# Moving the rotation ahead of the scan from VectorE to GpSimd, and adding the split-off exponentials' exponent in f32

## The chip, the cores and the metric

One core of one Trainium2 chip runs the kernel. The metric is the device time of one execution in microseconds, the median over several runs. Engines are named as in the profile: PE is TensorE's matmuls, PEld its weight loads, DVE is VectorE, ACT is ScalarE, POOL is GpSimd, SP is SyncE.

## The reference, cut to what matters

```
g = sigmoid((x * gate_w).sum(-1))                      # x: 2048 x 1024, bf16
a = S5(x)      # diagonal complex state space, 1024 states: h[t] = Lam_bar*h[t-1] + B_bar x[t];
               # y = 2 Re(C h) + x*Dskip
b = MHA(x)     # 32 heads of 32, full softmax over 2048 keys, then @ wo
out = g*a + (1-g)*b
```

## The kernel before, in words

**Attention sets the beat.** The scores of 32 heads are worked off in 512 *bursts*. A burst is four heads of one group, 256 queries and 256 keys: eight score matmuls (`burst`, PE L1576) fill two PSUM slots of 1024 columns per partition, two exponentials on ACT (L1594) turn them into two bf16 tiles `pt`, and 16 small matmuls (`pv`, PE L1655) add the tiles' products with V into PSUM bank 6. There are three PSUM slots for scores, so that PE can run about one burst ahead of ACT. After every eight bursts `normalize` (DVE L1668, L1669) divides by the row sums.

**Everything else is filled in.** Projections for the next head group, the state space's input projection (`d_u`), its output projection (`d_c`) and the output projection (`d_out`) are *chains* of eight 512-column matmuls, four in each burst, all into the one PSUM bank 7. So a chain takes two bursts, and at its end VectorE copies bank 7 out (the evictions L1410, L1427, L1439, L1475, L1499). The next chain's first matmul waits for that copy, and PE's queue is in order: a late copy holds the next burst's scores too.

**The state space.** 32 *items*: four time chunks of 512 by eight blocks of 128 states. For each, two chains bring u (real and imaginary) into a buffer `ub`. The recurrence is complex; with the tables `Et` (cosine, sine) the input is first turned back, so that a real scan can follow, and the result is turned forward again (`item_ops`). An item of the kernel before is, all on VectorE: four bf16 products of `ub` and `Et` and two sums into f32 `ut` (L1341), two scans of 512 steps (L1350), a copy of the last column (L1353, not in the last chunk), and four products and two sums for the turn forward into `hp` (L1341). After eight items `carry` hands the state to the next chunk with six tiny operations on GpSimd (L1374).

**Exponentials on VectorE.** In some bursts the last 256 of the 1024 columns of the second slot are not done by ACT (which then runs L1591 on 768) but by VectorE and GpSimd. Such bursts come in pairs (bursts 0 and 2, or 4 and 6, of eight), worked off together as 512 columns (`x_ops`): L1585 on VectorE scales the score to a 32-bit fixed-point exponent for each burst; then L1611 on GpSimd takes the upper 16 bits as exponent field (`xe`), L1620 and L1614 on VectorE work out a cubic polynomial of the lower 16 bits, L1615 on GpSimd scales it to bf16 (`xp`), and L1618 on VectorE adds the two bit patterns. `x_pv` multiplies the result with V (L1635).

**The planner.** `build` goes through the bursts in order and writes each engine's whole instruction order beforehand. `t0` is a burst's planned start, 1.83 us after the one before (`PERIOD`); `dve_t` is the planned time up to which VectorE is filled. Items wait as a list `bg`, table and `C` scaling work (`table_ops`, `fold_ops`) as `bg2`, the exponentials' work as `xbg`; in each burst as many are issued as fit by their planned costs before the chain's copy. The next `u` chain is let in when few enough items are open (`items_done`). A pair of bursts is given to VectorE when the background lists are nearly empty (`X_MOST`). The semaphore waits follow from the order and from tokens for each buffer.

Of the kernel before, what the change touches and what calls it, by code (L numbers as in the profile page):

```python
# [935 lines left out]
X_UNITS = (9, 63)  # L936
X_MOST = 0.01
# [16 lines left out]
class FastPath:  # L954

    def __init__(self, nc, S, es, d, flag):
# [370 lines left out]
    def item_ops(self, j, ch, n):  # L1327
        dve, ub, tq, ut, ht = self.dve, self.ub, self.tq, self.ut, self.ht
        b = self.hp_of[ch]
        hp = self.hpb[b]  # L1330
# [8 lines left out]

        def tt(c, o, a, b, op, r, w):  # L1340
            ops.append((c, lambda: dve(lambda e: e.tensor_tensor(o, a, b, op), r, w)))  # L1341
        tt(0.335, t[0], ure, er, ALU.mult, [u0, Et], [k[0]])
        tt(0.335, t[1], uim, ei, ALU.mult, [u1, Et], [k[1]])
        tt(0.335, t[2], uim, er, ALU.mult, [u1, Et], [k[2]])
        tt(0.335, t[3], ure, ei, ALU.mult, [u0, Et], [k[3]])
        tt(0.6, ut[:, 0, :], t[0], t[1], ALU.add, k[0:2], [("ut", 0)])
        tt(0.6, ut[:, 1, :], t[2], t[3], ALU.subtract, k[2:4], [("ut", 1)])
        rr = self.pf[:, self.RR, j:j + 1].to_broadcast([128, 512])
        for ri in range(2):
            ops.append((1.29, lambda ri=ri: dve(lambda e: e.tensor_tensor_scan(ht[:, ri, :], rr, ut[:, ri, :], self.init[:, ri, j:j + 1], ALU.mult, ALU.add),  # L1350
                                                [("ut", ri), "init", ("pf", self.RR)], [("ht", ri)])))
        if ch < 3:
            ops.append((0.13, lambda: dve(lambda e: e.tensor_copy(self.hl[:, :, j], ht[:, :, 511]), [("ht", 0), ("ht", 1)], [("hl", j)])))  # L1353
# [248 lines left out]
    def x_ops(self, b):  # L1602
# [4 lines left out]
        bits = xp.bitcast(mybir.dt.int16)  # L1607
        w = 65536.0
        i2, p2 = [("xi", 0), ("xi", 1)], [("xp", 0), ("xp", 1)]
        dead = [("pf", i) for i in range(8, 21)] + ["iot", "ioth", "ioti"] + [("pw2", i) for i in range(2)] if b == 0 else []  # L1610
        self.pool(lambda e: e.tensor_scalar(self.xe, hi, 128.0, 0.0, ALU.mult, ALU.add), i2, ["xe"] + dead, "x_e")  # L1611

        def last():
            self.dve(lambda e: e.scalar_tensor_tensor(xq[:], xq[:], E1 / E3 * w * w, lo, ALU.add, ALU.mult), ["xq"] + i2, ["xq"], "x_q")  # L1614
            self.pool(lambda e: e.tensor_scalar(xp[:], xq[:], E3 / (w * w * w), E0, ALU.mult, ALU.add), ["xq"], p2, "x_p")  # L1615

        def out():
# [436 lines left out]
```

## Time and profile before

| what | value |
|---|---|
| median of 3 runs | 951.7 us (951.43 to 952.03) |
| the profiled execution's own time | 952.28 us |
| its span, first to last instruction | 950.5 us |
| granted TensorE clock, mean | 0.997 |
| busy: PE / ACT / DVE / POOL | 923.3 / 928.6 / 668.8 / 109.1 us |
| exponentials with 768 columns (L1591) | 114 |

The profile is of one execution. Busy time is a union, so instructions that overlap on one engine count once; a group's mean is of single instructions and holds the overlap. `idle before` is the engine's idle time right before a group's instructions, and the arrow names what ended it. In a window, the columns are the window's length and then, for each engine, busy microseconds and in brackets the number of instructions that begin there.

### The profile page before, as it was taken

What the parts mean: (1) busy time and instruction counts of PE and PEld (TensorE: products, weight loads), DVE (VectorE), ACT (ScalarE), POOL (GpSimd) and SP (SyncE); (2) the same over time, 40 slices, a digit from 0 to 9 for tenths busy, and PEclk for the clock granted to TensorE, in tenths of its full rate; (3) what the DMA queues carried; (4) which work ended last, traced back from release to release, by engine and by line L of the source; (5) the groups of instructions that cost most, each with busy time, mean ns of one, the idle gap of its engine ahead of it and who ended that gap; (6) DMA issues with size and microseconds to landing.
All of it is one profiled execution on the core that took longest, in us unless ns stands there. A gap on an engine that the chain in (4) does not pass through costs nothing.

```text
span 950.5 us, 33825 instructions
## 1 busy us (share of the span) xinstructions
PE 923.3 (97%) x15316; PEld 493.3 (52%) x15316; DVE 668.8 (70%) x1382; ACT 928.6 (98%) x1034; POOL 109.1 (11%) x154
## 2 busy tenths in 40 slices
PE   8899999999999999999999999999999999999996
PEld 4555644464444554555644655544645556444443
DVE  2788888889888767555688845588857455665664
ACT  6999999999999999999999999999999999999997
POOL 2000000000000220122200012200010222222220
PEclk9999999999999999999999999999999999999998
DMA  9668533320133102130022300133101214124312
GB/s 200 91 109 127 75 62 75 71 30 30 38 73 71 31 8 60 46 80 16 8 52 52 71 30 27 51 83 63 41 16 41 74 38 126 47 79 125 111 60 72
DMA packets 157092, 60.90 MB, mean 64 GB/s; under 512 B 145680, under 2 KB 145680, under 8 KB 156944
## 3 DMA queue, kind: packets, MB, share of 16 engines
q1 hardware_dynamic: 154784, 58.16, 27.5%
q8 instruction: 121, 1.98, 0.9%
q10 hardware_dynamic: 2160, 0.53, 0.3%
q14 instruction: 27, 0.22, 0.1%
HBM read 16.79 MB, written 12.58 MB: 31 GB/s over the span
## 4 chain that ended last, share of the span: by engine, by line
ACT 52%; PE 41%; DVE 4%; SPq 1%; DMA 1%; issue 1%; DVEq 0%
ACT f_pt L1594 45%; PE f_ps L1655 10%; PE f_ps L1462 9%; PE f_ps L1576 7%; PE f_ps L1493 5%; PE f_ps L1403 4%; PE f_ps L1421 2%; ACT f_OT L1594 2%; ACT f_Et L1594 2%; PE f_ps L1433 2%; ACT f_cT_re L1594 2%; ACT f_cT_im L1594 2%; DVE f_xT L1499 1%; SPq L1053 1%; DVE f_Ag L1475 1%; DMA f_xT<-in_A_x_dram 1%
## 5 line engine op out<-in xcount | busy, mean ns | idle before, releaser
L1594 ACT ACTIVATE f_pt<-f_ps 128x1024 bf16<-128x1024 f32 x830 | 775.8, 1164 | 6.1 <-PE f_ps L1576 2.1
L1655 PEld LDWEIGHTS f_ps<-f_V,f_pt 128*128 128x128 bf16 x7324 | 214.6, 96 | 98.8 <-issue 97.3
L1655 PE MATMUL f_ps<-f_V,f_pt 128*128 128x33 bf16 x7324 | 262.9, 178 | 0.2 <-ACT f_pt L1594 0.2
L1576 PE MATMUL f_ps<-f_Q,f_K 32*128 32x256 bf16 x4096 | 203.3, 273 | 13.9 <-ACT f_pt L1594 3.2
L1576 PEld LDWEIGHTS f_ps<-f_Q,f_K 32*128 32x128 bf16 x4096 | 60.7, 92 | 200.7 <-ACT f_pt L1594 173.9
L1433 PE MATMUL f_ps<-f_xT,f_wb 128*128 128x512 bf16 x512 | 131.0, 377 | 1.4 <-DVE f_pf L1224 0.4
L1403 PE MATMUL f_ps<-f_xT,f_wb 128*128 128x512 bf16 x464 | 119.2, 379 | 0.2
L1611 POOL TENSOR_SCALAR f_pf<-f_xi 128x512 int16<-128x512 int16 x57 | 63.8, 1119 | 407.7 <-DVE f_xi L1585 402.0
L1591 ACT ACTIVATE f_pt<-f_ps 128x768 bf16<-128x768 f32 x114 | 96.7, 848 | 1.1 <-DVE f_xi L1585 1.1
L1350 DVE TENSOR_TENSOR_SCAN f_ht<-f_pf,f_init,f_ut 128x512 bf16<-128x512 f32 x64 | 80.8, 1274 | 0.0
L1462 PE MATMUL f_ps<-f_cT_re,f_hp 128*128 128x512 bf16 x192 | 72.6, 378 | 0.6
L1462 PE MATMUL f_ps<-f_cT_im,f_hp 128*128 128x512 bf16 x192 | 72.6, 378 | 0.0
L1493 PE MATMUL f_ps<-f_wb,f_OT 128*128 128x512 bf16 x220 | 62.6, 379 | 1.4
L1421 PE MATMUL f_ps<-f_wb,f_xT 128*128 128x128 bf16 x896 | 59.2, 219 | 0.1
L1433 PEld LDWEIGHTS f_ps<-f_xT,f_wb 128*128 128x128 bf16 x512 | 40.4, 96 | 33.9 <-issue 1.5
L1585 DVE TENSOR_SCALAR f_xi<-f_ps 128x256 int32<-128x256 f32 x114 | 47.5, 417 | 14.2 <-PE f_ps L1576 13.3
L1614 DVE SCALAR_TENSOR_TENSOR f_xq<-f_xq,f_xi 128x512 f32<-128x512 f32 x57 | 55.9, 980 | 1.9
L1668 DVE RECIPROCAL f_rc<-f_ps 128x8 f32<-128x8 f32 x63 | 13.1, 208 | 62.4 <-PE f_ps L1635 41.0
L1403 PEld LDWEIGHTS f_ps<-f_xT,f_wb 128*128 128x128 bf16 x464 | 36.2, 96 | 30.0
L1439 DVE CAST f_ub<-f_ps 128x512 bf16<-128x512 f32 x48 | 33.2, 692 | 26.2 <-PE f_ps L1433 26.2
L1475 DVE TENSOR_SCALAR f_Ag<-f_ps,f_gcol 128x512 f32<-128x512 f32 x32 | 24.0, 751 | 38.3 <-PE f_ps L1462 38.3
L1421 PEld LDWEIGHTS f_ps<-f_wb,f_xT 128*128 128x128 bf16 x896 | 50.4, 97 | 1.0
(148 smaller groups left out, 893.4 us busy)
## 6 DMA issues: line engine op xcount, KB each, us to landing
ag_scratch<-f_Ag SPq DMA_DIRECT2D x32, 256.0 KB, 2.3
f_hp<-ag_scratch SPq DMA_DIRECT2D x32, 256.0 KB, 2.9
f_wb<-in_B_wqkv_dram SPq DMA_DIRECT2D x21, 256.0 KB, 4.1
out_dram<-f_xT SPq DMA_DIRECT2D x16, 256.0 KB, 2.0
f_wb<-in_B_wo_dram SPq DMA_DIRECT2D x2, 768.0 KB, 4.3
f_OT<-f_On SPq DMA_TRANSPOSE x63, 2.3
f_wb<-in_B_wqkv_dram ACTq DMA_DIRECT2D x2, 256.0 KB, 4.2
f_wb<-in_A_B_re_dram SPq DMA_TRANSPOSE x32, 3.3
```

What stands on the lines that cost most here:

```text
L1350: ops.append((1.29, lambda ri=ri: dve(lambda e: e.tensor_tensor_scan(ht[:, ri, :], rr, ut[:, ri, :], self.init[:, ri, j:j + 1], ALU.mult, ...
L1403: mms.append((1, lambda e, f, l, a=a: e.matmul(ps[:, bank, :], w[:, g % 2, part, a, :], xT[:, a, 512 * ch:512 * (ch + 1)], start=f, stop=l ...
L1421: m = e.matmul(ps[:, bank, 128 * q:128 * (q + 1)], xT[:, a, 128 * kt:128 * (kt + 1)], w[:, g % 2, 2, a, :], start=(a == 0), stop=(a == 7))
L1433: mms.append((1, lambda e, f, l, a=a: e.matmul(ps[:, 7, :], bT[:, (2 * n + ri) % 3, a, :], xT[:, a, 512 * ch:512 * (ch + 1)], start=f, sto ...
L1462: mms.append((1, lambda e, f, l, j=j, ri=ri: e.matmul(ps[:, 7, :], hp[:, ri, j, cols], cT[ri][:, j, 512 * cb:512 * (cb + 1)], start=f, sto ...
L1493: mms.append((1, lambda e, f, l, j=j: e.matmul(ps[:, 7, :], OT[:, j, 256 * qb + 128 * r:256 * qb + 128 * (r + 1)], wo[j][0][:, 512 * cb:51 ...
L1576: m = e.matmul(ps[:, 2 * sl[h // 2] + h % 2, 256 * kl:256 * (kl + 1)], K[32 * h:32 * h + 32, g % 2, 128 * kt:128 * (kt + 1)], Q[32 * h:32 ...
L1591: self.S.op("act", lambda e, s=s, p=p: e.activation(flat(self.tile[p]), flat(ps[:, 2 * s:2 * s + 2, :]), ACT.Exp, scale=SCALE), reads=[("S ...
L1594: self.act(lambda e, s=s, p=p: e.activation(self.tile[p], ps[:, 2 * s:2 * s + 2, :], ACT.Exp, scale=SCALE), [("S", s)], [("pt", p)], "exp")
L1611: self.pool(lambda e: e.tensor_scalar(self.xe, hi, 128.0, 0.0, ALU.mult, ALU.add), i2, ["xe"] + dead, "x_e")
L1614: self.dve(lambda e: e.scalar_tensor_tensor(xq[:], xq[:], E1 / E3 * w * w, lo, ALU.add, ALU.mult), ["xq"] + i2, ["xq"], "x_q")
L1655: m = e.matmul(ps[:, 6, o:o + 33], self.tile[p][:, h2, 256 * kl + 128 * qt:256 * kl + 128 * (qt + 1)], V[:, g % 2, 2 * i + kl, h, :], star ...
```

## The change

Its description in a few words: "SSM rotation ahead of the scan on GpSimd as a second planned queue; 170 blocks of exps on VectorE from burst 108 on; exponent added in f32, bits last". In the code:

1. `item_ops` is split. `pre_ops` holds the four products and two sums ahead of the scan and gives them to GpSimd, with `tq` as the only scratch: product, product, sum into `ut`'s first half, product, product, difference into its second half. `item_ops` keeps the scans, the copy and the turn forward on VectorE; the products of the turn forward now go to `hp`, to a new scratch `tp` (in `pf`, where `xe` was) and in place into `ht`.
2. The planner gets a second time line, `pool_t`, with 1.3 us for each of the six operations (`POOL_TT`). Operations are issued in order while they fit before the burst's end; a sum waits in the plan until the scan of the item before is planned (`scanned`), since `ut` is single. An item joins VectorE's list `bg` when its six are planned. The `u` chains are now let in by `pre_done`, not `items_done`, and table work carries the burst from which it may run.
3. In `x_ops` the exponent field is no longer made on GpSimd: VectorE multiplies the upper 16 bits and adds them to the polynomial in f32 (a third operation of the L1614 kind), and one GpSimd operation scales and writes the 16-bit pattern. L1611 and L1618 go.
4. The bursts that are given to VectorE stand in a list, `X_PLAN`, in place of the rule with `X_MOST`; VectorE's choice among the three lists is by the earliest start.

```diff
-X_UNITS = (9, 63)
-X_MOST = 0.01
+POOL_TT = 1.3
+X_PLAN = (168, 172, 176, 180, 184, 188, 204, 208, 212, 216, 220, 224, 228, 232, 236, 240, 244, 248, 252, 296, 300, 304, 308, 312, 316, 320, 324, 328, 332, 376, 380, 400, 404, 408, 412, 416, 420, 424, 428, 432, 436, 440, 444, 448, 452, 456, 460, 464, 468, 472, 476, 480, 484, 488, 492, 496, 500,)
...
-    def item_ops(self, j, ch, n):
...
-        tt(0.335, t[0], ure, er, ALU.mult, [u0, Et], [k[0]])
-        tt(0.335, t[1], uim, ei, ALU.mult, [u1, Et], [k[1]])
-        tt(0.335, t[2], uim, er, ALU.mult, [u1, Et], [k[2]])
-        tt(0.335, t[3], ure, ei, ALU.mult, [u0, Et], [k[3]])
-        tt(0.6, ut[:, 0, :], t[0], t[1], ALU.add, k[0:2], [("ut", 0)])
-        tt(0.6, ut[:, 1, :], t[2], t[3], ALU.subtract, k[2:4], [("ut", 1)])
+    def pre_ops(self, j, ch, n):
...
+        def tt(o, a, b, op, r, w, add=False):
+            ops.append((POOL_TT, lambda: self.pool(lambda e: e.tensor_tensor(o, a, b, op), r, w), add))
+        t = [tq[:, 0, :], tq[:, 1, :]]
+        k = [("tq", 0), ("tq", 1)]
+        tt(t[0], ure, er, ALU.mult, [u0, Et], [k[0]])
+        tt(t[1], uim, ei, ALU.mult, [u1, Et], [k[1]])
+        tt(ut[:, 0, :], t[0], t[1], ALU.add, k, [("ut", 0)], True)
+        tt(t[0], uim, er, ALU.mult, [u1, Et], [k[0]])
+        tt(t[1], ure, ei, ALU.mult, [u0, Et], [k[1]])
+        tt(ut[:, 1, :], t[0], t[1], ALU.subtract, k, [("ut", 1)], True)
+        return ops
...
-        tt(0.335, t[0], hre, er, ALU.mult, [("ht", 0), Et], [k[0]])
-        tt(0.335, t[1], him, ei, ALU.mult, [("ht", 1), Et], [k[1]])
-        tt(0.335, t[2], hre, ei, ALU.mult, [("ht", 0), Et], [k[2]])
-        tt(0.335, t[3], him, er, ALU.mult, [("ht", 1), Et], [k[3]])
...
+        tt(h0, hre, er, ALU.mult, [("ht", 0), Et], [hk[0]] + hw)
+        tt(tp, him, ei, ALU.mult, [("ht", 1), Et], ["tp"] + dead)
+        tt(h1, hre, ei, ALU.mult, [("ht", 0), Et], [hk[1]] + hw)
+        tt(him, him, er, ALU.mult, [("ht", 1), Et], [("ht", 1)])
+        tt(h0, h0, tp, ALU.subtract, [hk[0], "tp"], [hk[0]])
+        tt(h1, h1, him, ALU.add, [hk[1], ("ht", 1)], [hk[1]])
...
-        self.pool(lambda e: e.tensor_scalar(self.xe, hi, 128.0, 0.0, ALU.mult, ALU.add), i2, ["xe"] + dead, "x_e")
 
         def last():
-            self.dve(lambda e: e.scalar_tensor_tensor(xq[:], xq[:], E1 / E3 * w * w, lo, ALU.add, ALU.mult), ["xq"] + i2, ["xq"], "x_q")
-            self.pool(lambda e: e.tensor_scalar(xp[:], xq[:], E3 / (w * w * w), E0, ALU.mult, ALU.add), ["xq"], p2, "x_p")
-
-        def out():
-            self.dve(lambda e: e.tensor_tensor(bits[:], self.xe, bits[:], ALU.add), ["xe"] + p2, p2, "x_out")
+            self.dve(lambda e: e.scalar_tensor_tensor(xq[:], hi, 128.0 / X_K, xq[:], ALU.mult, ALU.add), i2 + ["xq"], ["xq"], "x_q")
+            self.pool(lambda e: e.tensor_scalar(bits, xq[:], X_K, 128.0 * (E0 + 126.0), ALU.mult, ALU.add), ["xq"], p2, "x_p")
             self.x_done.add(b)
...
-            if p % 4 == 0 and X_UNITS[0] <= p // 8 < X_UNITS[1]:
-                if sum(c for c, *_ in self.bg + self.bg2) < X_MOST:
-                    self.x_plan(p // 8, X_AT[p // 4 % 2])
+            if p % 4 == 0 and p in X_PLAN:
+                self.x_plan(p // 8, X_AT[p // 4 % 2])
...
-                            u_ok = ri == 1 or (self.items_done >= n - (3 if n < 18 else 1) and hp_free)
+                            u_ok = ri == 1 or (self.pre_done >= n - (3 if n < 18 else 1) and hp_free)
...
+            self.t1 = t0 + period
+            while self.pre:
+                n, j, ch, ready, ops = self.pre[0]
+                if n < 8 and n not in self.tabled:
+                    break
+                c, f, add = ops[0]
+                if add and len(self.scanned) < n:
+                    break
+                st = max(self.pool_t, ready, t0, self.scanned[n - 1] if add and n else 0.0)
+                if st + c > self.t1 + 0.3:
+                    break
+                f()
+                ops.pop(0)
+                self.pool_t = st + c
+                if not ops:
...
+                    self.bg += [(c, f, n) for c, f in self.item_ops(j, ch, n)]
```

More of the change, by code (lines that the diff above doesn't have):

```diff
@@ L1606, in x_ops @@
         hi = xi.bitcast(mybir.dt.int16)[:, 1::2]
[L1607 removed]
+        bits = xp.bitcast(mybir.dt.int16)[:]
         w = 65536.0
         i2, p2 = [("xi", 0), ("xi", 1)], [("xp", 0), ("xp", 1)]
[L1610 to L1611 removed]
         def last():
[L1614 to L1618 removed]
+            self.dve(lambda e: e.scalar_tensor_tensor(xq[:], hi, 128.0 / X_K, xq[:], ALU.mult, ALU.add), i2 + ["xq"], ["xq"], "x_q")
+            self.pool(lambda e: e.tensor_scalar(bits, xq[:], X_K, 128.0 * (E0 + 126.0), ALU.mult, ALU.add), ["xq"], p2, "x_p")
             self.x_done.add(b)
[L1620 to L1622 removed]
+        return [(0.66, 0.0, lambda: self.dve(lambda e: e.scalar_tensor_tensor(xq[:], lo, E2 / E3 * w, lo, ALU.add, ALU.mult), i2, ["xq"], "x_q")),
+                (0.7, 0.0, lambda: self.dve(lambda e: e.scalar_tensor_tensor(xq[:], xq[:], E1 / E3 * w * w, lo, ALU.add, ALU.mult), ["xq"] + i2, ["xq"], "x_q")),
+                (0.7, 0.0, last)]
     def x_pv(self, b):
@@ L1754, in build @@
                 if n == 1:
-                    self.xbg += [[c, wait, f] for c, wait, f in self.x_ops(b)]
+                    self.xbg += [(c, f) for c, _, f in self.x_ops(b)]
             q0, q1 = self.quarters[p]
@@ L1758, in build @@
             for b in self.x_when.get(p, ()):
-                assert b in self.x_done, p
+                while b not in self.x_done:
+                    self.xbg.pop(0)[1]()
                 self.x_pv(b)
@@ L1853, in build @@
-                if not (self.bg or self.bg2):
+                now = max(self.dve_t, t0 + 0.3)
+                todo = [(max(now, self.pre_t.get(src[0][2], 0.0) if src is self.bg else 0.0), k, src) for k, src in enumerate((self.xbg, self.bg, self.bg2)) if src and not (k == 2 and len(src[0]) > 2 and src[0][2] > p)
+                        and not (k == 1 and self.bg2 and src[0][2] not in self.tabled)]
+                if not todo:
                     break
-                src = self.bg if self.bg and (self.bg[0][2] in self.tabled or not self.bg2) else self.bg2
```

65 lines of the change are left out of this document (29 added, 36 removed).

## The prediction

> **What bounds the kernel now.** I read the page's busy shares and its chain of waits first:
>
> ```profile
> PE 923.3 (97%) x15316; PEld 493.3 (52%) x15316; DVE 668.8 (70%) x1382; ACT 928.6 (98%) x1034; POOL 109.1 (11%) x154
> ...
> ACT 52%; PE 41%; DVE 4%; SPq 1%; DMA 1%; issue 1%; DVEq 0%
> ```
>
> ACT and PE are both nearly full, and the chain alternates between them; VectorE, which the change relieves, holds 4% of it. So the table of windows matters more than the mean: whose time is full where. The first seven windows are bursts 16 to 31, 32 to 47, 48 to 63, 64 to 79, 80 to 95, 112 to 127 and 256 to 287 (the start of a burst is the start of its first exponential), all without VectorE exponentials; in the last every second burst has them.
>
> ```profile
> core 0: us, PE busy (x) PEld busy (x) DVE busy (x) ACT busy (x) POOL busy (x), PEclk, DMA share, GB/s
> 39.80:69.90 30.10, 29.66 (x530) 15.45 (x526) 24.77 (x68) 30.01 (x35) 0.00 (x0) 1.00 0.54 86
> 69.90:99.60 29.70, 29.70 (x588) 17.94 (x585) 25.24 (x51) 29.70 (x33) 0.00 (x0) 1.00 0.81 124
> 99.60:129.10 29.50, 29.41 (x562) 17.46 (x563) 25.26 (x51) 29.50 (x33) 0.00 (x0) 1.00 0.43 60
> 129.10:158.30 29.20, 28.73 (x451) 13.70 (x448) 24.74 (x51) 29.20 (x34) 0.00 (x0) 1.00 0.38 79
> 158.30:187.60 29.30, 28.53 (x452) 13.47 (x450) 26.00 (x52) 29.30 (x33) 1.68 (x6) 1.00 0.36 79
> 216.90:246.30 29.40, 29.13 (x466) 14.61 (x467) 26.42 (x53) 29.40 (x34) 0.00 (x0) 1.00 0.08 25
> 477.80:536.20 58.40, 57.37 (x950) 29.61 (x946) 51.39 (x110) 58.40 (x66) 0.00 (x0) 1.00 0.34 70
> 770.00:800.00 30.00, 29.85 (x531) 17.66 (x528) 16.52 (x33) 29.29 (x35) 6.95 (x8) 1.00 0.24 76
> ```
>
> Without VectorE exponentials ACT is busy every microsecond and VectorE 82 to 90%; with them PE is full (29.85 of 30.00) and VectorE 55%. Nowhere does VectorE set the pace, but in the first kind of window it has only 3 to 5 us left in 30, and GpSimd is empty. The waits' view bounds what relief alone can bring:
>
> ```profile
> PEld f_ps L1576 <- ACT f_pt L1594: 173.9, 418, 1.2
> ...
> PEld f_ps L1493 <- DVE f_xT L1499: 2.7, 16, 0.2
> ...
> PEld f_ps L1462 <- DVE f_Ag L1475: 2.2, 13, 0.2
> ...
> PEld f_ps L1576 <- DVE f_K L1146: 2.0, 4, 0.7
> ```
>
> PE waits for VectorE some 7 us in all, most of it in bits of 0.2 us, and 173.9/418 = 0.42 us at a time for ACT: that is PE's spare time in a burst, and it swallows copies of bank 7 that are late by less.
>
> **Part 1: the exponentials' number.** The description speaks of 170 blocks from burst 108 on. The list in the code holds 57 starts from burst 168 on, each for two bursts, so 114 blocks; following the old rule through its planner gives the same 57 starts, and the row says x114 too:
>
> ```profile
> L1594 ACT ACTIVATE f_pt<-f_ps 128x1024 bf16<-128x1024 f32 x830 | 775.8, 1164 | 6.1 <-PE f_ps L1576 2.1
> L1591 ACT ACTIVATE f_pt<-f_ps 128x768 bf16<-128x768 f32 x114 | 96.7, 848 | 1.1 <-DVE f_xi L1585 1.1
> ```
>
> ACT and PE therefore get exactly the work they had. No term of the sum comes off them.
>
> **Part 2: exponent in f32.** The rows that it touches, with those of part 3:
>
> ```profile
> L1350 DVE TENSOR_TENSOR_SCAN f_ht<-f_pf,f_init,f_ut 128x512 bf16<-128x512 f32 x64 | 80.8, 1274 | 0.0
> L1611 POOL TENSOR_SCALAR f_pf<-f_xi 128x512 int16<-128x512 int16 x57 | 63.8, 1119 | 407.7 <-DVE f_xi L1585 402.0 <-PE f_ps L1576 5.6
> L1614 DVE SCALAR_TENSOR_TENSOR f_xq<-f_xq,f_xi 128x512 f32<-128x512 f32 x57 | 55.9, 980 | 1.9
> L1620 DVE SCALAR_TENSOR_TENSOR f_xq<-f_xi 128x512 f32<-128x512 uint16 x57 | 39.5, 692 | 1.9
> L1615 POOL TENSOR_SCALAR f_xp<-f_xq 128x512 bf16<-128x512 f32 x57 | 35.2, 617 | 35.4 <-DVE f_xq L1614 35.4
> L1439 DVE CAST f_ub<-f_ps 128x512 bf16<-128x512 f32 x48 | 33.2, 692 | 26.2 <-PE f_ps L1433 26.2
> L1618 DVE TENSOR_TENSOR f_xp<-f_pf,f_xp 128x512 int16<-128x512 int16 x57 | 23.8, 418 | 11.8 <-POOL f_xp L1615 11.8
> L1341 DVE TENSOR_TENSOR f_ut<-f_tq 128x512 f32<-128x512 bf16 x32 | 21.9, 684 | 0.0
> L1319 DVE TENSOR_TENSOR f_OT<-f_OT 128x512 f32<-128x512 f32 x32 | 20.5, 684 | 0.0
> L1341 DVE TENSOR_TENSOR f_tq<-f_ub,f_Et 128x512 bf16<-128x512 bf16 x48 | 18.3, 419 | 0.0
> L1305 DVE SCALAR_TENSOR_TENSOR f_cT_re<-f_cT_re,f_pf,f_OT 128x512 bf16<-128x512 bf16 x16 | 11.9, 747 | 0.0
> L1303 DVE TENSOR_SCALAR f_OT<-f_cT_im,f_pf 128x512 f32<-128x512 bf16 x16 | 7.7, 481 | 0.0
> ```
>
> A pair of bursts costs VectorE 0.69 + 0.98 + 0.42 = 2.09 us now. After, three operations of the L1620 kind: 3 x 0.69 = 2.07 us, or 2.7 if the new one, with its strided 16-bit input, takes L1614's 0.98 each time. GpSimd loses 1.12. VectorE is at 55% there and the result is read four bursts later, so: zero, off the path. Its cover is VectorE's 13 idle us in 30; the worst case, 57 x 0.6 = 34 us, stays under that. Below zero is excluded too: the waits' view has no row in which PE waits for L1618.
>
> **Part 3: the rotation on GpSimd.** An item takes 4 x 0.42 + 2 x 0.68 = 3.04 us off VectorE, 97 us over 32 items. GpSimd gets 192 operations with two inputs of 512. The trace has none of that size, but it shows what happens when both engines want SBUF, in two places of the timeline:
>
> ```profile
> 403.15 0.69 DVE L1620 SCALAR_TENSOR_TENSOR f_xq<-f_xi 128x512 f32<-128x512 uint16 x1
> 403.20 1.12 POOL L1611 TENSOR_SCALAR f_pf<-f_xi 128x512 int16<-128x512 int16 x1 [4.80 <-DVE f_xi L1585]
> 403.87 0.98 DVE L1614 SCALAR_TENSOR_TENSOR f_xq<-f_xq,f_xi 128x512 f32<-128x512 f32 x1
> ...
> 541.39 0.76 DVE L1341 TENSOR_TENSOR f_tq<-f_ht,f_Et 128x512 bf16<-128x512 bf16 x2
> 541.57 1.32 POOL L1374 TENSOR_TENSOR f_cm<-f_hl,f_W 128x8 f32<-128x8 f32 x4 [64.29 <-DVE f_hl L1353]
> 542.07 0.76 DVE L1341 TENSOR_TENSOR f_ut<-f_ht,f_Et 128x512 bf16<-128x512 bf16 x2
> 542.86 0.47 POOL L1374 TENSOR_TENSOR f_init<-f_cm 128x8 f32<-128x8 f32 x2
> 543.06 0.69 DVE L1427 CAST f_V<-f_ps 128x512 bf16<-128x512 f32 x1 [0.23 <-PE f_ps L1421]
> ```
>
> First place: L1620 ends at 403.84; the GpSimd operation ends at 404.32, 0.48 later; L1614 starts at 403.87 and takes 0.98, which is 0.29 more than L1620. They ran in turns, each waiting for the other. Second place: beside four bf16 products, GpSimd's four tiny ones take 0.32 each (1.29 to the next group), the pace of the products themselves (541.39 to 542.07 for two); beside a copy out of PSUM two take 0.47, or 0.23 each. So an operation of VectorE with two SBUF inputs and one of GpSimd go one for one, and a copy from PSUM blocks nobody. [...] It speaks against this change: by it a rotation on GpSimd isn't beside VectorE but between its operations.
>
> The price of one: one input of 512 held VectorE off till 404.32, 0.48 us of turn. Two inputs cost between 0.48 (read together) and 2 x 0.62 = 1.23 (twice the L1615 row); I take 2 x 0.48 = 0.95, as the two products' inputs are read by an engine that took 0.48 for one. Of these turns some fall beside PSUM copies (0.69 every other burst) or idle time; in a window where VectorE is full I count five sixths as lost to it, **0.8 us an operation** (ends 0.4 and 1.2). [...]
>
> Now by windows: VectorE before, plus what the new order moves (counted in both planners' orders and priced by the rows above), plus 0.8 us for each GpSimd operation there, against the window's length, which ACT sets.
> - 64 to 79: 24.74; twelve rotation operations go (-6.1), two table operations, six scalings and four of the L1305 kind come forward from later (+1.4 +2.9 +3.0): 25.9. Sixteen on GpSimd: +12.8. 38.7 against 29.2: **9.5 late**.
> - 80 to 95: 26.0; -6.1 and nine table operations less (-6.1), but ten L1305, eight scalings and two products come: +0. Fifteen: +12.0. 38.0 against 29.3: **8.7 late**.
> - 16 to 31: six rotation operations (-3.0) and two products less (-0.8), three table operations more (+2.0): 24.77 - 1.8 + 9 x 0.8 = 30.2 against 30.1, zero. 32 to 47: twelve (-6.1), a scan and its copy (-1.4) less, three table operations and two products more (+2.9): 25.24 - 4.6 + 10 x 0.8 = 28.6 against 29.7, zero. 48 to 63: six less (-3.0), a scan, its copy and a table operation more (+2.1): 25.26 - 0.9 + 5 x 0.8 = 28.4 against 29.5, zero.
> - 112 to 127: the 29 fold operations that came forward (-18.0), six rotation operations (-3.0) and three copies of bank 7 (-2.2) go; four scans, thirteen products, six copies and two small ones come (+15.0): 26.42 - 8.2 + 13 x 0.8 = 28.6 against 29.4, zero.
> - 256 to 287: 35 rotation operations (-17.6), a scan and its copy (-1.4), six products and an L1618 (-2.9) go: 51.39 - 21.9 + 31 x 0.8 = 54.3 against 58.4, zero; 336 to 367 alike.
>
> What is late is VectorE's queue, and in it the copy of bank 7; behind that stand PE's next chain, the next scores and ACT. Nothing gives it back, since the order is fixed and ACT was full. That is 18 us. In the other windows the sum fits but not each chain: where the turn forward falls into one chain, 6 x 0.34 + 3 x 0.95 + 0.69 = 5.6 us stand against 3.66 and PE's spare 2 x 0.42, 1.1 late; for some 20 items outside the two windows, at a third of the time, 7 us. Together +25.
>
> Small things at nothing: `carry`'s six tiny operations stand behind rotations on GpSimd's queue (three times, some us, their reader is bursts away); L1615 likewise where a stretch of exponentials begins. No DMA is added, and the loads for `u` chains hang on the same evictions, SP's order with them.
>
> **The rivals.**
> 1. *Hidden.* The turns fall beside PSUM copies and VectorE's waits, 0.2 us or less of each is lost ((29.2 - 25.9)/16), and nothing is late. For: VectorE idles 3 to 13 us per window. Against: the one-for-one rows. Time: 952, within 1.5 us.
> 2. *Faster.* Rival 1's condition, and VectorE, 97 us lighter, copies out earlier, so that PE's 7 us of waiting for it go. Decides: lost turn under 0.2 us. For: those waits are real. Against: they lie mostly in windows with VectorE exponentials, where no rotation runs. Time: at best 951.7 - 7 = 945, likely 948.
> 3. *GpSimd becomes the bound.* Its operation costs its turn, 0.95 to 1.2, its own fixed 0.23 and the wait for one VectorE operation, about 0.65 as a mean of 0.42, 0.75 and 1.27: 1.83 to 2.1 against a burst's 1.83, for one operation in each burst. At 2.1 each item is 6 x 0.27 = 1.6 late, scans wait for `ut`, copies behind them: 26 items outside the two windows, +42 on top: 1019. It decides at 1.83 us an operation.
>
> **How the numbers follow.** The chance of the forecast, late copies by turns, is 0.62; hidden 0.12, faster 0.08, GpSimd the bound 0.18. The sum stands on the profiled execution, 952.28 us, 0.6 above the median; I put it on the median: 951.7 + 25 = 977. With 0.4 an operation the two windows are 3.1 and 2.7 late, and no bunching: 957. With 1.2, windows 16 to 63 give 7, 64 to 95 give 31, 112 to 127 gives 4, the two late double windows 8 each, with the 7: +65, 1017. The forecast's own range is 957 to 1017; mine reaches to 951 for the hidden case and 1020 for the third rival, leaving some 0.17 out. Within 0.2% (1.9 us, about what a measurement of this kernel can tell from no change) is 0.12, faster 0.08, slower 0.80.
>
> **What would show it.** L1591 still x114. GpSimd some 200 us busier, its new operations at a mean above 1 us. VectorE's products of the turn forward and scans longer than 0.42 and 1.27 where GpSimd runs. Bursts 64 to 95 at 2.4 us and not 1.83, with idle ACT and PE waiting for DVE evictions; windows with VectorE exponentials unchanged. Wrong: scans and products at their old means, or bursts 64 to 95 at 1.83. Right in kind but rival 3: DVE scans waiting for POOL `ut`, and windows 256 to 287 and 336 to 367 late as well.

## The result: 952 to 1040 us

Four runs of each kernel on the same chip: before 951.87 us (951.43 to 952.79), after 1040.39 us (1038.36 to 1041.63). The ratio is 1.0918, with a 95% interval of 1.0902 to 1.0933: 88 us slower, where 25 were forecast. One execution of the write-only kernel below, 1061 us at a granted clock of 0.752 where its nine others took 951 to 954, is in no ratio.

The page of the kernel after, its profiled execution at 1039.70 us: the span, the busy shares and the chain.

```profile
span 1038.0 us, 33880 instructions
...
PE 946.9 (91%) x15316; PEld 502.1 (48%) x15316; DVE 687.5 (66%) x1190; ACT 933.9 (90%) x1034; POOL 299.9 (29%) x289
...
PE 62%; DVE 23%; ACT 12%; issue 2%; SPq 1%; DMA 1%; DVEq 0%
```

The span grew by 87.5 us. PE ran as many matmuls as before, 15316, but was busy 946.9 - 923.3 = 23.6 us longer: the same work at a lower granted clock, 0.963 as a mean against 0.997. Its idle time went from 950.5 - 923.3 = 27.2 to 1038.0 - 946.9 = 91.1 us, which is the other 63.9. VectorE's share of the chain went from 4% to 23%, ACT's from 52% to 12%.

The table of windows of the kernel after. The rows are bursts 16 to 31, 32 to 47, 48 to 63, 64 to 79, 80 to 95, 112 to 127, 128 to 143, 144 to 159, 256 to 287 and 336 to 367, and last a stretch with VectorE exponentials.

```profile
core 0: us, PE busy (x) PEld busy (x) DVE busy (x) ACT busy (x) POOL busy (x), PEclk, DMA share, GB/s
...
40.00:72.40 32.40, 29.85 (x530) 15.56 (x527) 27.63 (x61) 30.11 (x35) 16.65 (x12) 1.00 0.46 78
72.40:106.70 34.30, 30.02 (x589) 18.11 (x587) 27.00 (x45) 29.86 (x33) 13.78 (x11) 1.00 0.63 109
106.70:137.80 31.10, 29.56 (x562) 17.51 (x561) 27.03 (x48) 29.49 (x33) 5.63 (x4) 1.00 0.36 56
137.80:177.90 40.10, 31.34 (x454) 14.28 (x451) 37.40 (x46) 30.42 (x33) 23.90 (x18) 0.91 0.28 57
177.90:224.60 46.70, 34.45 (x451) 14.73 (x448) 38.75 (x56) 30.14 (x34) 19.80 (x20) 0.78 0.34 61
253.60:287.80 34.20, 30.06 (x504) 16.39 (x504) 26.06 (x37) 29.87 (x33) 22.00 (x16) 0.95 0.07 13
287.80:326.90 39.10, 32.21 (x465) 15.04 (x461) 26.87 (x36) 29.79 (x33) 18.99 (x15) 0.87 0.20 45
326.90:361.80 34.90, 31.24 (x469) 15.49 (x466) 22.06 (x37) 29.50 (x33) 14.80 (x16) 0.90 0.23 58
534.80:608.00 73.20, 62.16 (x952) 31.70 (x949) 48.51 (x66) 59.65 (x66) 42.93 (x34) 0.91 0.27 55
694.60:766.50 71.90, 60.82 (x949) 32.04 (x945) 46.85 (x62) 59.40 (x65) 43.23 (x35) 0.93 0.29 57
827.00:855.00 28.00, 27.92 (x476) 15.72 (x471) 15.73 (x31) 27.50 (x33) 1.85 (x3) 1.00 0.21 64
```

The first five rows answer to 30.1, 29.7, 29.5, 29.2 and 29.3 us before, the sixth to 29.4, the ninth to 58.4; the trace of before has 29.3 for bursts 128 to 143 and for 144 to 159, and 58.4 for 336 to 367. So the losses are 2.3, 4.6, 1.6, 10.9, 17.4, 4.8, 9.8, 5.6, 14.8 and 13.5 us, 85.3 of the 87.5. Every window with rotation lost time. The last row has not: 28.00 us with 33 exponentials begun, 0.85 each, where the stretch of that kind shown of before has 30.00 with 35, 0.86 each. The row to look at is bursts 128 to 143: VectorE is busy 26.87 us of work that would fit the old 29.3, and the window takes 39.1. A sum by windows can't see that loss. Bursts 128 to 159, for which the prediction's list has no row, lost 15.4 us.

The groups of the kernel after that answer to those shown of before (mean ns behind the busy time, then the idle time ahead of the group):

```profile
L1338 POOL TENSOR_TENSOR f_tq<-f_ub,f_Et 128x512 bf16<-128x512 bf16 x96 | 123.0, 1297 | 86.1 <-DVE f_ub L1452 41.1 <-DVE f_Et L1323 40.7
L1338 POOL TENSOR_TENSOR f_ut<-f_tq 128x512 f32<-128x512 bf16 x64 | 88.0, 1375 | 158.1 <-DVE f_ht L1361 155.0
L1603 ACT ACTIVATE f_pt<-f_ps 128x768 bf16<-128x768 f32 x114 | 95.4, 837 | 1.2 <-DVE f_xi L1597 1.2
L1361 DVE TENSOR_TENSOR_SCAN f_ht<-f_pf,f_init,f_ut 128x512 bf16<-128x512 f32 x64 | 84.9, 1348 | 0.0
L1358 DVE TENSOR_TENSOR f_pf<-f_ht,f_Et 128x512 bf16<-128x512 bf16 x32 | 33.4, 1044 | 0.0
L1452 DVE CAST f_ub<-f_ps 128x512 bf16<-128x512 f32 x48 | 33.0, 687 | 28.2 <-PE f_ps L1446 28.1
L1320 DVE TENSOR_TENSOR f_OT<-f_OT 128x512 f32<-128x512 f32 x32 | 30.2, 989 | 0.0
L1365 DVE CAST f_hl<-f_ht 128x2 f32<-128x2 bf16 x24 | 17.2, 715 | 0.8
```

The turn forward's second product takes 1044 ns, not 419; a scan 1348, not 1274; the table operation L1320, not touched by the change, 989, not 684. The copies out of PSUM (L1452) stay at 687, against 692. The waiting goes the other way round than rival 3 had it: the scans' idle time is 0.0, but GpSimd waits 155 us for scans, because its sums need the one `ut` that the scan of the item before still reads.

What follows from that wait stands in the timeline of the kernel after (start, us, engine, line, operation):

```profile
170.52 2.45 DVE L1361 TENSOR_TENSOR_SCAN f_ht<-f_pf,f_init,f_ut 128x512 bf16<-128x512 f32 x2
...
171.94 1.98 POOL L1338 TENSOR_TENSOR f_ut<-f_tq 128x512 f32<-128x512 bf16 x1 [8.15 <-DVE f_ht L1361]
...
174.68 1.02 PE L1446 MATMUL f_ps<-f_xT,f_wb 128*128 128x512 bf16 x4 [0.38 <-DVE f_ub L1452]
175.35 1.37 DVE L1358 TENSOR_TENSOR f_pf<-f_ht,f_Et 128x512 bf16<-128x512 bf16 x1
...
176.51 1.22 POOL L1338 TENSOR_TENSOR f_ut<-f_tq 128x512 f32<-128x512 bf16 x1
176.64 1.38 DVE L1358 TENSOR_TENSOR f_hp<-f_ht,f_Et 128x512 bf16<-128x512 bf16 x1
...
177.81 2.50 POOL L1338 TENSOR_TENSOR f_tq<-f_OT,f_Et 128x512 bf16<-128x512 bf16 x2
177.94 1.37 DVE L1358 TENSOR_TENSOR f_ht<-f_ht,f_Et 128x512 bf16<-128x512 bf16 x1
179.23 1.37 DVE L1358 TENSOR_TENSOR f_hp<-f_hp,f_pf 128x512 bf16<-128x512 bf16 x1
...
181.25 0.68 DVE L1452 CAST f_ub<-f_ps 128x512 bf16<-128x512 f32 x1
...
182.07 1.86 PE L1446 MATMUL f_ps<-f_xT,f_wb 128*128 128x512 bf16 x4 [3.84 <-DVE f_ub L1452]
```

Read it in four steps. GpSimd's sum has waited 8.15 us for `ut` and starts at 171.94, when the first of the two scans has ended; so the operations behind it in GpSimd's queue stand beside the turn forward. Three products and a difference of the turn forward start at 175.35, 176.64, 177.94 and 179.23, 1.29 us apart, in turns with GpSimd; in the kernel before it was 0.34. Behind them in VectorE's queue stands the copy of bank 7, at 181.25, and PE waits 3.84 us for it. Then four matmuls that took 1.02 us before the wait take 1.86.

The last step is the clock, as the windows around it show it:

```profile
176.50:179.90 3.40, 1.74 (x30) 0.77 (x26) 3.40 (x4) 3.35 (x4) 3.31 (x3) 1.00 0.39 47
179.90:186.70 6.80, 4.63 (x35) 1.48 (x36) 4.38 (x10) 1.94 (x2) 0.41 (x1) 0.50 0.09 19
```

The granted clock is 0.50 for 6.8 us. Behind the start-up PE has 22 gaps of more than 1.2 us in this trace, 1.5 to 4.1 us each and 61.7 us together, about all of the added idle time (the kernel before has none); 15 of them are followed by half the clock, for 72 us in all. In these 61.7 us VectorE is busy with the turn forward for 39.2, with the awaited copies for 15.0 and with table and `C` scaling work, which is slowed as well (L1320 at 989 ns and not 684), for 10.1 (the ends of operations overlap).

### The profile page after: what moved, and what is told of

Same layout as the page of the kernel before. It is cut to its first block, busy times and chain, and to the rows that moved or that the text cites. A ratio compares the mean times of both kernels' runs of the same rounds, so it can differ in the third digit from the quotient of the medians.

```text
span 1038.0 us, 33880 instructions
## 1 busy us (share of the span) xinstructions
PE 946.9 (91%) x15316; PEld 502.1 (48%) x15316; DVE 687.5 (66%) x1190; ACT 933.9 (90%) x1034; POOL 299.9 (29%) x289
## 4 chain that ended last, share of the span: by engine, by line
PE 62%; DVE 23%; ACT 12%; issue 2%; SPq 1%; DMA 1%; DVEq 0%
PE f_ps L1662 15%; PE f_ps L1588 11%; ACT f_pt L1606 10%; PE f_ps L1474 10%; PE f_ps L1416 9%; PE f_ps L1446 7%; PE f_ps L1434 4%; PE f_ps L1505 4%; DVE f_hp L1358 4%; DVE f_ht L1361 3%; DVE f_pf L1358 3%; DVE f_ht L1358 2%; DVE f_OT L1320 2%; DVE f_ub L1452 2%; DVE f_hl L1365 1%
## 5 line engine op out<-in xcount | busy, mean ns | idle before, releaser
L1588 PE MATMUL f_ps<-f_Q,f_K 32*128 32x256 bf16 x4096 | 207.7, 278 | 9.0 <-ACT f_pt L1606 3.3
L1446 PE MATMUL f_ps<-f_xT,f_wb 128*128 128x512 bf16 x512 | 139.4, 396 | 25.9 <-DVE f_ub L1452 13.4
L1625 POOL TENSOR_SCALAR f_xp<-f_xq 128x512 int16<-128x512 f32 x57 | 35.3, 619 | 422.3 <-DVE f_xq L1624 369.6
L1338 POOL TENSOR_TENSOR f_tq<-f_ub,f_Et 128x512 bf16<-128x512 bf16 x96 | 123.0, 1297 | 86.1 <-DVE f_ub L1452 41.1
L1416 PE MATMUL f_ps<-f_xT,f_wb 128*128 128x512 bf16 x464 | 125.9, 395 | 17.9 <-DVE f_ub L1452 10.3
L1338 POOL TENSOR_TENSOR f_ut<-f_tq 128x512 f32<-128x512 bf16 x64 | 88.0, 1375 | 158.1 <-DVE f_ht L1361 155.0
L1603 ACT ACTIVATE f_pt<-f_ps 128x768 bf16<-128x768 f32 x114 | 95.4, 837 | 1.2 <-DVE f_xi L1597 1.2
L1361 DVE TENSOR_TENSOR_SCAN f_ht<-f_pf,f_init,f_ut 128x512 bf16<-128x512 f32 x64 | 84.9, 1348 | 0.0
L1446 PEld LDWEIGHTS f_ps<-f_xT,f_wb 128*128 128x128 bf16 x512 | 41.6, 98 | 63.7 <-issue 32.0
L1434 PE MATMUL f_ps<-f_wb,f_xT 128*128 128x128 bf16 x896 | 62.3, 225 | 8.6 <-DVE f_ub L1452 4.7
L1416 PEld LDWEIGHTS f_ps<-f_xT,f_wb 128*128 128x128 bf16 x464 | 37.1, 99 | 51.2 <-DVE f_ub L1452 10.7
L1434 PEld LDWEIGHTS f_ps<-f_wb,f_xT 128*128 128x128 bf16 x896 | 53.1, 101 | 10.3 <-DVE f_ub L1452 4.9
```

What stands on the lines that cost most here:

```text
L1338: ops.append((POOL_TT, lambda: self.pool(lambda e: e.tensor_tensor(o, a, b, op), r, w), add))
L1416: mms.append((1, lambda e, f, l, a=a: e.matmul(ps[:, bank, :], w[:, g % 2, part, a, :], xT[:, a, 512 * ch:512 * (ch + 1)], start=f, stop=l ...
L1434: m = e.matmul(ps[:, bank, 128 * q:128 * (q + 1)], xT[:, a, 128 * kt:128 * (kt + 1)], w[:, g % 2, 2, a, :], start=(a == 0), stop=(a == 7))
L1446: mms.append((1, lambda e, f, l, a=a: e.matmul(ps[:, 7, :], bT[:, (2 * n + ri) % 3, a, :], xT[:, a, 512 * ch:512 * (ch + 1)], start=f, sto ...
L1588: m = e.matmul(ps[:, 2 * sl[h // 2] + h % 2, 256 * kl:256 * (kl + 1)], K[32 * h:32 * h + 32, g % 2, 128 * kt:128 * (kt + 1)], Q[32 * h:32 ...
L1603: self.S.op("act", lambda e, s=s, p=p: e.activation(flat(self.tile[p]), flat(ps[:, 2 * s:2 * s + 2, :]), ACT.Exp, scale=SCALE), reads=[("S ...
```

## The experiments

The theory after this: a turn beside a product holds VectorE up for the 0.95 us that was forecast, but the time is lost by single late copies, which the wait for `ut` puts regularly behind a slowed turn forward, and PE's clock adds to each. The rivals: that the f32 exponent costs; that the new order costs without any turns; that GpSimd's writes, not its reads, are in the way; that the loss is VectorE's lost time itself, wherever it falls.

### The exponent alone

The kernel before with the new `x_ops` only:

```diff
-            self.dve(lambda e: e.tensor_tensor(bits[:], self.xe, bits[:], ALU.add), ["xe"] + p2, p2, "x_out")
+            self.dve(lambda e: e.scalar_tensor_tensor(xq[:], hi, 128.0 / X_K, xq[:], ALU.mult, ALU.add), i2 + ["xq"], ["xq"], "x_q")
+            self.pool(lambda e: e.tensor_scalar(bits, xq[:], X_K, 128.0 * (E0 + 126.0), ALU.mult, ALU.add), ["xq"], p2, "x_p")
```

> The kernel before with the exponent added in f32 alone (three VectorE operations and one on GpSimd per pair of bursts); the rotation stays on VectorE and the order of chains is the old one. Theory (the slowdown is the rotation's alone): 952 us, within 1 us; the third operation takes 0.69 us. Rival (the longer VectorE part of the exponentials is late in the windows that have them): 957 us or more, with bursts there over 1.81 us.

Measured 953.02 us against 952.63, ratio 1.0006 (0.9997 to 1.0015). The groups of this kernel:

```profile
L1617 DVE SCALAR_TENSOR_TENSOR f_xq<-f_xq,f_xi 128x512 f32<-128x512 f32 x57 | 39.4, 692 | 1.9
L1613 DVE SCALAR_TENSOR_TENSOR f_xq<-f_xi,f_xq 128x512 f32<-128x512 int16 x57 | 39.4, 692 | 1.9
```

The new operation takes 0.69 us, and the one that took 0.98 beside GpSimd's exponent field takes 0.69 too, now that the field is gone. Part 2 costs nothing.

### The order without the turns

The kernel after, with its GpSimd operations on 8 of 512 columns (the rotation is left out for the others; `ut` is cleared at the start):

```diff
-            ops.append((POOL_TT, lambda: self.pool(lambda e: e.tensor_tensor(o, a, b, op), r, w), add))
+            ops.append((POOL_TT, lambda: self.pool(lambda e: e.tensor_tensor(o[:, 0:8], a[:, 0:8], b[:, 0:8], op), r, w), add))
```

> The changed kernel with all its orders and waits, but GpSimd's 192 rotation operations work on 8 of 512 columns, so the rest of the rotation is left out. Theory (each operation's turn at SBUF holds VectorE's operations up, and with them the copy of bank 7): turns of some 0.1 us cost nothing, 952 to 957 us. Rival (the new order and its waits are slow: scans wait for GpSimd, single ut, chains let in too early): over 1000 us. If both count, in between.

Measured 952.72 us, ratio 1.0001 (0.9992 to 1.0010). Its page:

```profile
PE 890.2 (94%) x15095; PEld 493.5 (52%) x15316; DVE 590.0 (62%) x1190; ACT 928.6 (98%) x1034; POOL 103.6 (11%) x290
```

The order, the waits and the list cost nothing; and they gain nothing. VectorE is 668.8 - 590.0 = 79 us lighter than in the kernel before, and the time is the same: rival 2's gain isn't there even with the rotation all but free. (Some matmul records are missing here, x15095, so PE's busy time isn't compared.) Against this page the turns of the kernel after cost VectorE 687.5 - 590.0 = 97.5 us, 0.51 for each of 192 operations.

### The same operations on VectorE

Same places in the order, but issued to VectorE: `self.pool(` becomes `self.dve(` in that line.

> The changed kernel with the six operations of each rotation issued to VectorE at the very places where the planner had put them on GpSimd; nothing else differs. They cost VectorE 0.42 and 0.68 us each instead of one turn of about 1.2. Theory (a turn is lost to VectorE whole): faster than the changed kernel in spite of 97 us more work on VectorE: 960 to 985 us, since the planner left no place for them. Rival (VectorE's own load is what makes it late): slower than 1040 us.

Measured 961.49 us, ratio 1.0094 (1.0078 to 1.0109). The groups:

```profile
L1338 DVE TENSOR_TENSOR f_ut<-f_tq 128x512 f32<-128x512 bf16 x64 | 43.9, 685 | 0.4
L1338 DVE TENSOR_TENSOR f_tq<-f_ub,f_Et 128x512 bf16<-128x512 bf16 x96 | 39.2, 415 | 0.2
```

Here VectorE does the rotation itself, in an order planned without room for it, and the kernel is 79 us faster than with GpSimd. A product takes VectorE 0.42 us when it does it itself, and a turn of 0.95 when GpSimd does it beside a product. But VectorE's time alone doesn't explain the 79 us: it is busy for 666.7 us here, 76.7 more than with 8 columns, or 0.40 for each of the 192 operations, against 0.51 for a turn as a mean. That is 21 us between the two kernels; the rest is not VectorE's own time.

### Write only, and half the columns

GpSimd writes the same outputs at the same places but reads nothing (the rotation is left out):

```diff
-            ops.append((POOL_TT, lambda: self.pool(lambda e: e.tensor_tensor(o, a, b, op), r, w), add))
+            ops.append((POOL_TT, lambda: self.pool(lambda e: e.memset(o, 0.5), r, w), add))
```

> The changed kernel with GpSimd's 192 operations made into memsets of the same outputs behind the same waits, so the rotation is left out and GpSimd reads nothing. Theory (it is GpSimd's reading that takes turns with VectorE's second input): 952 to 957 us, products of the turn forward back at 0.42 us. Rival (any GpSimd operation of that size, its writes too, holds VectorE off): products longer by the memset's time, 970 us or more.

Measured 953.14 us, ratio 1.0003 (0.9993 to 1.0013). The groups:

```profile
L1338 POOL MEMSET f_tq<- 128x512 bf16 x128 | 64.5, 526 | 138.7 <-DVE f_ub L1452 71.3 <-DVE f_Et L1323 64.7
L1358 DVE TENSOR_TENSOR f_pf<-f_ht,f_Et 128x512 bf16<-128x512 bf16 x32 | 13.4, 419 | 0.0
L1365 DVE CAST f_hl<-f_ht 128x2 f32<-128x2 bf16 x24 | 6.8, 281 | 0.8
```

A full-size write of 526 ns leaves the products at 419 ns, as they were before the change, where GpSimd's products and sums, which read as well, have them at 1044: it is GpSimd's reads that take the turns.

Half the columns, `[:, 0:256]` in that line (the rotation of the other half left out):

> The changed kernel with GpSimd's rotation operations on 256 of 512 columns (the other half of the rotation is left out): turns of about 0.6 us, as long as the memsets of write_only, but reading SBUF. Theory (reads take turns; what is late by less than PE's spare 0.4 us a burst costs nothing): products of the turn forward longer than 0.42 us, and a loss of less than half of 88 us, 960 to 985. Rival (every lost microsecond of VectorE counts): 996, half of the loss. Rival (length alone, reads and writes alike): 953, as write_only.

Measured 965.55 us, ratio 1.0139 (1.0122 to 1.0156), at a clock of 0.999. The groups:

```profile
L1339 POOL TENSOR_TENSOR f_tq<-f_ub,f_Et 128x256 bf16<-128x256 bf16 x96 | 71.3, 757 | 99.2 <-DVE f_ub L1453 52.9 <-DVE f_Et L1324 41.8 <-POOL f_ut L1339 0.5
L1359 DVE TENSOR_TENSOR f_pf<-f_ht,f_Et 128x512 bf16<-128x512 bf16 x32 | 22.9, 717 | 0.0
```

The product's excess is 717 - 419 = 298 ns, against 625 at full size: half. The time lost is 13 us against 88: a seventh. So the price of a turn grows with its size, but the kernel's loss does not follow VectorE's lost time.

### How lateness becomes time

The dose by itself: the kernel before, GpSimd's rotation not in it, with one, two or four scans of 1.28 us added ahead of the copy of bank 7 in 22 bursts.

```diff
+LATE = set(range(33, 160, 8)) | set(range(257, 289, 8)) | set(range(337, 369, 8))
...
+                if p in LATE:
+                    for _ in range(2):
+                        self.dve(lambda e: e.tensor_tensor_scan(self.xp[:], ...), ["xq", "init", ("pf", self.RR)], [("xp", 0), ("xp", 1)], "late")
```

> The kernel before with one extra scan of 1.27 us ahead of the copy of bank 7 at the end of 22 chains (late2 had two, late4 four). If a late copy costs its lateness less PE's spare time and the clock falls only after stalls of some 2 us: 22 x 0.5 to 0.9, 963 to 973 us, with a granted clock over 0.99. If the loss is in proportion to the extra work, half of late2's: 981 us.

> The kernel before with two extra scans of 1.27 us on VectorE ahead of the copy of bank 7 at the end of 22 chains, in windows without VectorE exponentials: the copy is late by 2.5 us. If a late copy costs what is left of it after PE's spare time (some 1 us), and no more: 22 x 1.5 = 33, 985 us. If PE's clock falls after such a stall: 1000 us or more, with a granted clock under 0.99.

> The same with four extra scans: late by 5.1 us. Without an effect of the clock 22 x 4.1 = 90, 1042 us, so just 57 more than late2. With PE's clock halved for 3.4 to 6.8 us after a stall of some 4 us, another 1.5 to 3 us each: 1075 to 1110 us, with a granted clock of 0.95 or less.

Measured: one scan 966.29 us against 952.75, ratio 1.0141 (1.0124 to 1.0158); two 1010.35 against 952.68; four 1088.78 against 952.68 (one execution each for the last two, which are 58 and 136 us from the kernel before). For each late copy: 1.28 us late cost 13.5 / 22 = 0.6 us, 2.56 cost 2.6, 5.1 cost 6.2. Of the first scan slack takes up half; beyond it each us of lateness costs more than a us: the second scan 2.0 for 1.28, the third and fourth 3.6 for 2.56. The surplus goes with the granted clock, 0.997, 0.976 and 0.938. In the timeline of the kernel with two scans, two of the late places:

```profile
146.43 0.81 PE L1435 MATMUL f_ps<-f_xT,f_wb 128*128 128x512 bf16 x3 [2.45 <-DVE f_ub L1441]
...
163.27 1.49 PE L1435 MATMUL f_ps<-f_xT,f_wb 128*128 128x512 bf16 x3 [2.63 <-DVE f_OT L1441]
```

Nearly the same wait, and three matmuls take 0.81 us after the first and 1.49 after the second. The windows of seven bursts around these two:

```profile
141.87:156.68 14.81, 11.84 (x204) 6.12 (x204) 13.24 (x24) 12.97 (x16) 0.00 (x0) 1.00 0.30 67
158.49:174.52 16.03, 12.87 (x203) 6.36 (x205) 12.58 (x23) 13.07 (x15) 0.00 (x0) 0.89 0.28 62
```

Seven bursts take 7 x 29.2 / 16 = 12.8 us without a late copy. The loss of clock in the second, 0.11 of 16.03, is one piece of 3.4 us at 0.5, and it costs 16.03 - 14.81 = 1.2 us, of which 0.2 is the longer wait. By 1.0 to 1.2 a piece the 72 us at half the clock in the kernel after come to 21 to 25 us of its 88, near the 23.6 by which PE is busier.

### Moving the rotation off the turn forward

`ut` doubled, so that GpSimd's sums needn't wait for the scan of the item before; that there is room, it is held in bf16, which changes the scans' input precision and nothing else of the work (GpSimd's sums take 1363 ns against 1375):

```diff
+        uo = ut.bitcast(BF)[:, :, 512 * (n % 2):512 * (n % 2 + 1)]
...
-        tt(ut[:, 0, :], t[0], t[1], ALU.add, k, [("ut", 0)], True)
+        tt(uo[:, 0, :], t[0], t[1], ALU.add, k, [("ut", n % 2, 0)], True)
```

> The changed kernel in the same order, with ut in bf16 and two of them in the same bytes, so that GpSimd's sums for an item needn't wait for the scans of the item before. Theory (the wait on the single ut releases GpSimd just when VectorE begins the turn forward, so that up to six turns fall together ahead of one copy of bank 7): turns spread out, 975 to 1010 us. Rival (the sum of the turns counts, wherever they fall): 1035 to 1045.

Measured 1011.08 us, ratio 1.0621 (1.0604 to 1.0639). A wait and two groups of this kernel, from two views:

```profile
POOL f_ut L1339 <- DVE f_ht L1362: 64.7, 7, 32.8
```

```profile
L1362 DVE TENSOR_TENSOR_SCAN f_ht<-f_pf,f_init,f_ut 128x512 bf16<-128x512 f32 x64 | 95.2, 1507 | 0.0
...
L1359 DVE TENSOR_TENSOR f_pf<-f_ht,f_Et 128x512 bf16<-128x512 bf16 x32 | 27.6, 864 | 0.0
```

GpSimd's waits for scans fell from 25 to 7. Its turns now fall beside scans, 1507 ns and not 1348, and less beside the turn forward, 864 and not 1044. A turn taken beside a scan of 1.27 us stands against an operation that is long already; beside a product of 0.34 the same turn nearly quadruples it, to 1.29. That is 29 us back, with a third of the loss gone and no operation fewer. PE's gaps of over 1.2 us are 17 now, 45.4 us together, and VectorE is in the turn forward for 18.5 of them, not 39.2. It doesn't cure it: 58 us stay.

The other way: the plan told that a turn forward takes longer, so that VectorE is given less of it ahead of a copy. In `item_ops`' helper the planned price of one operation goes from 0.335 to 0.5; no instruction is changed, only its place.

```diff
-            ops.append((0.335, lambda: dve(lambda e: e.tensor_tensor(o, a, b, op), r, w)))
+            ops.append((0.5, lambda: dve(lambda e: e.tensor_tensor(o, a, b, op), r, w)))
```

> The changed kernel with the planner's price of a product or sum of the turn forward at 0.50 instead of 0.335 us, nearer to the 0.8 that they take beside GpSimd, so that fewer of them stand ahead of a copy of bank 7. Instructions and turns are the same. Theory (lateness of single copies costs, not VectorE's lost time): 990 to 1025 us. Rival (the turns' sum costs): 1035 to 1045.

Measured 1005.76 us, ratio 1.0558 (1.0541 to 1.0576). Its group:

```profile
L1358 DVE TENSOR_TENSOR f_pf<-f_ht,f_Et 128x512 bf16<-128x512 bf16 x32 | 33.0, 1032 | 0.0
```

The turns are as dear as in the kernel after, 1032 against 1044 ns, and VectorE is busy 682.2 us against 687.5; yet 35 us come back. Fewer of these operations stand in front of a copy: PE has 15 gaps of over 1.2 us, 35.0 us together, with VectorE in the turn forward for 20.0. This falls against the rival that VectorE's lost time itself is the loss.

### More exponentials on VectorE

The description spoke of 170 blocks from burst 108 on; the code has 114. With 83 starts from burst 108 on (166 blocks), on 8 columns and on the full kernel:

```diff
-X_PLAN = (168, 172, 176, 180, 184, 188, 204, 208, ...
+X_PLAN = (108, 112, 116, 120, 124, 128, 132, 136, ...
```

> cols8 (rotation on 8 columns, so free) with the list of bursts for VectorE's exponentials grown from 57 starts to 83 (166 blocks, from burst 108 on): what the relief of VectorE could be spent on. Theory (ACT gives up 0.18 us a block, but PE is the next bound, 1.80 instead of 1.83 us a burst): 52 more blocks save 3 to 5 us, 948 to 950. Rival (ACT sets the whole time): 52 x 0.32 = 17 us, 936.

> The changed kernel with the same list of 83 starts, so the change as it was described: whole rotation on GpSimd, 166 blocks. Theory: VectorE and the turns are in the same windows now, so it is no faster than the changed kernel, 1035 to 1075 us. Rival (the described version differs in kind, more exponentials pay for the turns): under 1020.

Measured, on 8 columns: 950.35 us, ratio 0.9977 (0.9967 to 0.9987); on the full kernel 1042.39 (one execution). The same 110 us in both kernels with 8 columns, first without the added blocks, then with them:

```profile
217.00:327.00 110.00, 105.55 (x1740) 55.94 (x1766) 60.83 (x126) 110.00 (x122) 13.16 (x47) 1.00 0.18 45
```

```profile
217.00:327.00 110.00, 108.97 (x1793) 57.60 (x1790) 91.97 (x180) 108.27 (x122) 17.98 (x51) 1.00 0.21 45
```

With the blocks PE is at 108.97 of 110.00: ACT is relieved, and PE is the next bound at once. So 52 more blocks are worth 2.4 us when the rotation costs nothing, and with the rotation none is seen. No kernel here, that computes the whole reference, is faster than the one before.

## Why the prediction was wrong in size

**What held.** L1603 is x114, and the kernel with the new exponent alone is level: parts 1 and 2 were zero. GpSimd is 190.8 us busier, its operations take 1.30 and 1.38 us, and they go one for one with VectorE's two-input operations. The turn was taken as 0.95 us; the products' starts give 1.29 - 0.34 = 0.95. Copies from PSUM lost nothing (687 ns against 692). The stretch with VectorE exponentials alone is unchanged. Slower was right, at 1040 against a range to 1020.

**What was too dear.** "Five sixths lost", 0.8 us an operation: VectorE lost 0.51. By the prediction's own sum, a smaller loss should have made a faster kernel than forecast. It was 63 us slower, so the fault is not in the price.

**The step that failed: the balance by windows.** The prediction added up VectorE's work in 16 bursts, held it against the window's length, and called a sum that fits zero, with 7 us for bunching "at a third of the time". Bursts 64 to 95 came to +28.3 us for the forecast 18, all others to some +59 for the forecast 7. What counts is not the window but the one copy in two bursts: PE has some 2 x 0.42 us to spare, and in the timeline its wait for one copy behind a turn forward is 3.84. And the third of the time was a mis-sized chance. The prediction treated GpSimd's place as free against VectorE's; but with a single `ut` its sums wait for the scans, and when they are let go (171.94 in the timeline) the rest of its queue runs beside the turn forward that comes behind the scans. The timeline shows that tie, and undoing it by the doubled `ut`, or making room for it by the planner's price, is worth 29 and 35 us.

**The term that was missing: PE's clock.** The prediction counted a late copy at the time it is late. The runs with added scans show 2.6 us for 2.56, with half of the first scan's 1.28 taken up by slack, and 6.2 for 5.1; the piece at half the clock costs 1.0 to 1.2 us. For the kernel after that is some 23 us, by the busier PE (23.6) and by the pieces (21 to 25).

**The rivals.** Rival 1 (hidden) is what the kernel with 8 columns and the write-only one show, and fails on the reads. Rival 2 fails even without turns: with VectorE 79 us lighter, nothing came off. Rival 3 had the windows 256 to 287 and 336 to 367 late, which they are, by 14.8 and 13.5 us, but not by its mechanism: scans wait for nothing, idle 0.0. Its time, 1019, was nearer than the forecast's for a reason that wasn't its own. (Its 0.65 us for a wait, "as a mean of 0.42, 0.75 and 1.27", is 0.81 if each counts alike.)

**Open.** No experiment splits the 58 us that remain with the doubled `ut`. In its trace, PE's 45.4 us of gaps find VectorE in scans for 0.8 us, in the turn forward for 18.5, and in table and `C` scaling work beside GpSimd for 14.6, so scans right ahead of a copy are hardly what is left. Nor was a kernel tried that plans GpSimd's operations beside PSUM copies only.

## What to carry to other kernels

Work that two engines can only do in turns isn't moved off the first by giving it to the second: price the turn (0.95 us beside a product, 0.51 as a mean) beside the operation itself (0.42 to 0.69, 0.40 as a mean), before the move. Then follow the latest single hand-over to the engine that sets the pace, not the sum over a window, and ask which wait ties the second engine's operations to the first's: a single buffer can align them at the worst place. Where PE stands still for some 2 us or more (12 of 22 places with two scans, all 22 with four), count its clock as a cost of its own, behind the stall.

## What the runs showed of the hardware that was not expected

**The clock falls after gaps shorter than its piece.** In the kernel after, the 15 stretches at a granted clock of 0.50 that follow 15 of its 22 gaps are nine of 3.41 us and six of twice that. With two added scans, gaps of 1.8 to 2.6 us were followed by half the clock at 12 of 22 places; with four, gaps of 4.4 to 5.3 us at all 22; on half the columns, gaps of 1.2 to 1.9 us at none of 6.

Why the same gap may or may not be followed by it can be read from the traces. In the kernel after, all 31 changes of the clock, over 884 us, lie whole multiples of 3.413 us apart, so they give a grid of windows. The grid of the kernel with two scans, laid over its two late copies shown, the first pair of rows around the first, the second around the second:

```profile
141.98:145.40 3.42, 2.00 (x39) 1.00 (x35) 3.25 (x6) 3.42 (x5) 0.00 (x0) 1.00 0.19 39
145.40:148.81 3.41, 2.38 (x31) 1.15 (x32) 2.46 (x4) 1.57 (x3) 0.00 (x0) 1.00 0.36 82
...
159.05:162.47 3.42, 1.59 (x28) 0.72 (x26) 3.35 (x6) 3.34 (x4) 0.00 (x0) 1.00 0.11 22
162.47:165.88 3.41, 2.61 (x28) 1.16 (x30) 2.07 (x3) 0.53 (x1) 0.00 (x0) 0.50 0.35 74
```

The grid cuts the first gap near its middle: PE idles 1.42 us of one window and 1.03 of the next, and the clock stays. It cuts the second near its end: 1.83 us are idle in one window, and the next is at half the clock. In the kernel after, behind the start-up and ahead of the last 25 us, every window at full clock with 1.70 us or more of PE's idle time is followed by half the clock, 15 of them, and none with 1.66 or less. With two scans it is 12 windows with 1.59 us or more, and one with 1.78 that isn't followed; on half the columns no window exceeds 1.56. So about half of one window idle, 1.70 us of 3.41, was enough in the kernel after; an estimate from the two numbers is that for a gap between some 1.7 and 3.4 us it is luck where the grid cuts it.

**A copy of two columns can wait as long as a large one.** The copy of the scan's last column (L1365) took 169 ns before and 715 in the kernel after, 546 more, where a product of 512 columns (L1358 into `pf`) took 625 more; it took still 281 beside write-only operations, where the products of 512 columns lost nothing (419).
